# Walking the streamed operand and the accumulator of a matmul in blocks of 16 words, from the last to the first

## The chip, the core and the metric

The kernel runs on one core of a Trainium2 chip. A core has a matrix engine (TensorE, PE in the profile, with its weight loads shown apart as PEld), VectorE (DVE), ScalarE (ACT), GpSimd (POOL) and a queue for DMA transfers (SP). On-chip memory has 128 partitions; so has the accumulator memory of the matrix engine, which has eight banks of 512 words of 32 bits in each partition. The metric is the device time of one execution in microseconds, as the median of several runs.

## What is computed

A linear attention without a softmax is followed by two matrix products with a softplus between them, all in 32-bit floats:

```python
# q, k, v: (8, 8, 576, 64)
kv = np.einsum('bhsd,bhse->bhde', k, v)
out = np.einsum('bhsd,bhde->bhse', q, kv)
rms = np.sqrt(np.mean(out * out, axis=-1, keepdims=True) + 1e-06)
attn = out / rms * g_norm
x = attn.transpose(0, 2, 1, 3).reshape(4608, 512)
h = x @ w_in                                    # w_in (512, 2048)
g = np.maximum(h, 0.0) + np.log1p(np.exp(-np.abs(h)))
return g @ w_out                                # w_out (2048, 512)
```

## The kernel before

**Precision by three terms.** TensorE runs in the format `fp32r`, which keeps fewer bits than a 32-bit float. So each operand of the two large products is split into a high part, a scaled low part and a third term that combines both (on ScalarE and VectorE), and three matmuls, added up in the accumulator, stand for one of full precision. That is the loop `for m in range(3)` that appears in each product.

**Two halves of the span.** In the first 357 us the attention is computed and, beside it, the first part of `d_ff` in the plain form: for blocks of 384 tokens, the first product at L858 (twelve matmuls of 384 columns), softplus, split, and the second product at L865 (nine matmuls of 512 columns). From about 357 us on, the rest of `d_ff` is computed in a form that works on blocks of 512 tokens and pairs of 128-row chunks of `d_ff`; this is where the change is.

**The seven-product form.** For a block of 512 tokens and a pair of chunks the first product is a product of 2 x 2 blocks. `wide_step` computes it with seven products of sums and differences of blocks in place of eight (the scheme of Strassen and Winograd). `product(u, q)` is one of the seven: `u` names the combination of the weights (`forms[p][f]`) and of the tokens (`unit_slots`), `q` one of four quarters X, V, Y, Z of two accumulator banks, each 256 words of a partition (`place(q)`). A product is six matmuls at L1060, three terms by two halves of the contraction, each with weights of 128 x 128 and a streamed operand of 128 x 256. The weights differ in every matmul, so each has its own weight load. There are 48 steps of seven products with six matmuls each: 2016 matmuls.

**Who reads the quarters.** Between the products, ScalarE copies a quarter to another one (L1101, L1105) so that the next product adds onto it, or to on-chip memory (L1084); ScalarE applies softplus to finished quarters (L1087), and VectorE adds two quarters and a kept one (L1109). The result is split into its three terms (L1117, L1120, L1123) and goes to the second product at L1130: groups of three matmuls with 512 columns, whose weights are the token data (`gv`, `g`) and whose streamed operand is the split `w_out` (`pieces` and others).

**The streamed operand of L1060.** The token combinations are made by `units_of`: loaded from DRAM, subtracted where needed (L984), split by L1020, L1023 and L1026 into a tile of three terms, up to two combinations, two contraction halves and 256 tokens. The tiles are called `units`, `early` and `turned` in the profile. `dst.tile[:, m, v, kd]` is 256 neighbouring words of each partition. The weights are in `pieces`, `w12` to `w14` and `half0` to `half2`. Two small unused tiles, `gap0` and `gap1`, shift the tiles behind them.

**What sets the order.** The kernel describes its work as tasks for the class `Plan`, each with an engine, an estimated duration (710 ns for a product, 700 for three matmuls of L1130), a position, what it waits for and which buffers it takes and gives back. `Plan.order` simulates this list once and writes out all instructions in the order found. The durations are constants in the code. Each engine then works through its own queue in that order, with semaphores between engines.

Of the kernel before, what the change touches and what calls it, by code (L numbers as in the profile page):

```python
# [18 lines left out]
P = 128  # L19
# [7 lines left out]
def shaped(x, shape, dtype):  # L27

    n = 1
    for d in shape[1:]:  # L30
        n *= d
    words = n // 2 if dtype == BF16 else n
    x = x[:, :words]
    if x.dtype != dtype:
        x = x.bitcast(dtype)
    names = "abcdef"[:len(shape) - 1]
    if len(names) < 2:
        return x
    return x.rearrange(f"r ({' '.join(names)}) -> r {' '.join(names)}", **dict(zip(names, shape[1:])))


class Slot:
# [159 lines left out]
def kernel(  # L202
# [24 lines left out]
    nc = tc.nc  # L227
# [80 lines left out]
    minus_r = space("gv1", 4 * WIDE, False, F32R)[:, 3 * NT:3 * NT + P]  # L308
    early = space("early", 2 * PIECE, False)
    kvs = [shaped(early[:, 2 * PIECE - (i + 1) * NP * D:2 * PIECE - i * NP * D], [P, NP, D], F32) for i in range(2)]  # L310
    tails = [shaped(space("g0", 2 * WIDE, False)[:, i * H * D:], [P, H, D], F32) for i in range(2)]

    rings = dict(m=8, n=9, e=4, xv=2, gv=2, g=2, raw=1, rawb=1, sq=1, tail0=1, tail1=1, qa=1, xb=1, x=2, r=2,
# [12 lines left out]
    def new(s, shape, dtype=F32):  # L326
# [4 lines left out]
        elif r == "ab":  # L331
            s.tile = banks[:, 2 * i:2 * i + 2]
        elif bank is not None:
            s.tile = shaped(banks[:, bank], shape, dtype)
        elif r == "xv":
            s.tile = shaped(units[:, 3 * i:3 * i + 3].rearrange("r a b -> r (a b)"), shape, dtype)
# [701 lines left out]
    def wide_step(k):  # L1038
        ph, n, p = STEPS[k]
        ab, gv = slot("ab"), slot("gvp")  # L1040
        b = starts[k]
# [6 lines left out]
        def place(q):  # L1048
            return ab.tile[:, q // 2, q % 2 * HW:(q % 2 + 1) * HW]
# [3 lines left out]
        def product(u, q):  # L1053
            f, i = PRODUCTS[u]
            w = forms[p][f].tile
            dst, v = unit_slots[ph, n, u]
            for m in range(3):
                for kd in range(2):
                    at = i * 2 * P + kd * P
                    nc.tensor.matmul(place(q), lhsT=w[:, m, at:at + P], rhs=dst.tile[:, m, v, kd] if u < 6 else dst.tile[:, m, kd],  # L1060
                                     start=(u == 0 and not m and not kd), stop=(m == 2 and kd == 1), skip_group_check=True)

        def multiply(u, q, after, pos, take=(), follows=None):
            f = PRODUCTS[u][0]
            give = [unit_slots[ph, n, u][0]] if last else []
            if final and u in (2, 3, 5, 6):
                give.append(forms[p][f])
            return add("PE", 710, lambda: product(u, q), unit_done[ph, n, u] + forms_done[p][f] + list(after), pos, take, give,
                       follows=follows)
# [19 lines left out]
        def begin():  # L1089
            new(ab, None)  # L1090
            product(0, X)
# [168 lines left out]
```

## Time and profile before

| | |
|---|---|
| Median of 3 runs | 868.56 us (868.41 to 869.19) |
| Span of the profiled execution | 867.5 us, 17041 instructions |
| TensorE, matmuls busy | 853.9 us (98%), 6464 matmuls |
| TensorE, weight loads busy | 760.3 us (88%) |
| VectorE, ScalarE, GpSimd busy | 704.4, 521.3, 76.6 us |
| Matmuls of L1060 | 2016, 128 x 256, 282 to 283 ns recorded for each |
| Matmuls of L1130 | 1152, 128 x 512, 389 to 394 ns recorded for each |
| Moved by DMA | 167.07 MB, mean 193 GB/s |

The profiled execution is one of its own; the profile gives its span, from the first to the last instruction, and the runs behind the median are timed as whole executions. The recorded time of one matmul runs from its start to the modelled arrival of its last result. Consecutive matmuls overlap, so the sum of the recorded times is larger than the time they take, and the distance from start to start is what a matmul costs in a row of them. A line of the timeline has the start in us from the span's start, the time from the first start to the last end of the instructions merged in it, the engine, the line, the operation, the tiles written and read, the shapes and the count. In a line of the waits stand who waited, for whom, the sum of the waiting in us, how often, and the longest.

### The profile page before, as it was taken

What the parts mean: (1) busy time and instruction counts of PE and PEld (TensorE: products, weight loads), DVE (VectorE), ACT (ScalarE), POOL (GpSimd) and SP (SyncE); (2) the same over time, 40 slices, a digit from 0 to 9 for tenths busy, and PEclk for the clock granted to TensorE, in tenths of its full rate; (3) what the DMA queues carried; (4) which work ended last, traced back from release to release, by engine and by line L of the source; (5) the groups of instructions that cost most, each with busy time, mean ns of one, the idle gap of its engine ahead of it and who ended that gap; (6) DMA issues with size and microseconds to landing.
All of it is one profiled execution on the core that took longest, in us unless ns stands there. A gap on an engine that the chain in (4) does not pass through costs nothing.

```text
span 867.5 us, 17041 instructions
## 1 busy us (share of the span) xinstructions
PE 853.9 (98%) x6464; PEld 760.3 (88%) x6464; DVE 704.4 (81%) x995; ACT 521.3 (60%) x980; POOL 76.6 (9%) x79
## 2 busy tenths in 40 slices
PE   7899999999999999999999999999999999999998
PEld 5678888898888999989999999998999899999996
DVE  7888898888788879798887798878788666788873
ACT  6866664445444467766667655654868555566654
POOL 0342223111113200000000000000000000000000
PEclk9999999999999999999999999999999999999999
DMA  9998998779773655436645546545364752777764
GB/s 278 285 242 230 244 262 255 172 224 234 211 188 114 180 175 166 145 108 209 210 156 164 168 151 205 188 144 170 122 201 140 230 165 91 241 236 241 242 190 126
DMA packets 239778, 167.07 MB, mean 193 GB/s; under 512 B 106320, under 2 KB 198736, under 8 KB 239696
## 3 DMA queue, kind: packets, MB, share of 16 engines
q1 hardware_dynamic: 239392, 165.86, 64.5%
q8 instruction: 50, 0.82, 0.4%
q14 instruction: 32, 0.26, 0.1%
q10 hardware_dynamic: 304, 0.13, 0.1%
HBM read 112.98 MB, written 52.95 MB: 191 GB/s over the span
## 4 chain that ended last, share of the span: by engine, by line
PE 94%; DVE 1%; ACT 1%; POOL 0%; issue 0%; ACTq 0%; DVEq 0%
PE banks L1130 31%; PE banks L1060 28%; PE banks L865 16%; PE banks L858 15%; PE banks L715 2%; PE banks L691 2%; PE banks L733 0%; DVE units L638 0%; DVE half L727 0%; PE banks L1224 0%; POOL roots L723 0%; DVE units L641 0%; DVE roots L719 0%; DVE m L459 0%; ACT units L635 0%
## 5 line engine op out<-in xcount | busy, mean ns | idle before, releaser
L1130 PE MATMUL banks<-pieces,gv 128*128 128x512 f32 x768 | 239.9, 394 | 0.0
L1130 PEld LDWEIGHTS banks<-pieces,gv 128*128 128x128 f32 x768 | 133.5, 189 | 18.4
L1130 PE MATMUL banks<-pieces,g_False 128*128 128x512 f32 x384 | 149.4, 389 | 0.0
L858 PE MATMUL banks<-units,pieces 128*128 128x384 f32 x768 | 145.4, 337 | 0.0
L865 PE MATMUL banks<-pieces,gv 128*128 128x512 f32 x576 | 144.9, 396 | 0.0
L858 PEld LDWEIGHTS banks<-units,pieces 128*128 128x128 f32 x768 | 135.5, 188 | 4.8
L865 PEld LDWEIGHTS banks<-pieces,gv 128*128 128x128 f32 x576 | 106.1, 188 | 20.3
L1060 PEld LDWEIGHTS banks<-units,pieces 128*128 128x128 f32 x840 | 112.8, 190 | 6.8 <-ACT banks L1105 0.4
L1060 PE MATMUL banks<-units,pieces 128*128 128x256 f32 x840 | 117.1, 282 | 0.0
L880 ACT ACTIVATE half<-banks 128x384 f32<-128x384 f32 x64 | 31.4, 491 | 98.2 <-PE banks L858 98.0
L1120 DVE TENSOR_TENSOR gv<-g_True,gv 128x1024 fp32r<-128x1024 f32 x47 | 57.5, 1223 | 37.8 <-ACT gv L1117 37.8
L1130 PEld LDWEIGHTS banks<-pieces,g_False 128*128 128x128 f32 x384 | 72.2, 188 | 15.9
L1060 PEld LDWEIGHTS banks<-units,w 128*128 128x128 f32 x504 | 67.8, 190 | 3.9 <-ACT banks L1105 0.2
L1060 PE MATMUL banks<-units,w 128*128 128x256 f32 x504 | 70.7, 282 | 0.0
L723 POOL TENSOR_TENSOR roots<-roots,half 128x8 f32<-128x8 f32 x36 | 62.3, 1731 | 3.0
L1123 DVE SCALAR_TENSOR_TENSOR g_False<-gv 128x1024 fp32r<-128x1024 f32 x47 | 57.6, 1225 | 1.5
L1109 DVE TENSOR_TENSOR g_True<-banks,g_True 128x512 f32<-128x512 f32 x48 | 33.1, 690 | 30.5 <-PE banks L1060 24.5
L1087 ACT ACTIVATE g_True<-banks 128x256 f32<-128x256 f32 x96 | 36.6, 382 | 32.8 <-PE banks L1060 32.2
L1023 DVE TENSOR_TENSOR units<-loads,units 128x1024 fp32r<-128x1024 f32 x42 | 51.2, 1219 | 6.3 <-ACT units L1020 6.3
L925 ACT ACTIVATE m<-banks 128x512 f32<-128x512 f32 x72 | 42.1, 595 | 19.8 <-PE banks L1130 13.8
L1026 DVE SCALAR_TENSOR_TENSOR units<-units 128x1024 fp32r<-128x1024 f32 x42 | 51.4, 1224 | 1.8
L869 DVE TENSOR_TENSOR gv<-half,gv 128x384 fp32r<-128x384 f32 x64 | 35.4, 553 | 20.6 <-ACT gv L882 19.9
(115 smaller groups left out, 1260.5 us busy)
## 6 DMA issues: line engine op xcount, KB each, us to landing
loads<-x SPq DMA_DIRECT2D x180, 128.0 KB, 2.6
part<-m SPq DMA_DIRECT2D x72, 256.0 KB, 2.9
m<-part SPq DMA_DIRECT2D x72, 256.0 KB, 3.2
loads<-form SPq DMA_DIRECT2D x45, 256.0 KB, 3.2
form<-loads SPq DMA_DIRECT2D x36, 256.0 KB, 3.0
raw<-in_moe_w_in_dram SPq DMA_DIRECT2D x16, 512.0 KB, 4.5
loads<-in_k_dram SPq DMA_DIRECT2D x32, 256.0 KB, 4.1
loads<-in_v_dram SPq DMA_DIRECT2D x32, 256.0 KB, 4.4
```

The costliest lines, as they stand in the source:

```text
L723: nc.gpsimd.tensor_tensor(out=r.tile, in0=r.tile, in1=half, op=ALU.pow)
L858: nc.tensor.matmul(hp, lhsT=w_in.tile[:, i, kd * P:(kd + 1) * P], rhs=xv.tile[:, i, kd], start=(m == 0), stop=(m == 3 * KD - 1))
L865: nc.tensor.matmul(mine[i].tile, lhsT=gv.tile[:, m, i * P:(i + 1) * P], rhs=w_out.tile[:, m], start=(c == cs[0] and m == 0), stop=(c == cs ...
L869: nc.vector.tensor_tensor(out=gv.tile[:, 1], in0=g.tile, in1=gv.tile.bitcast(F32)[:, 0], op=ALU.subtract)
L925: a = add("ACT", 690 if ph == LAST else 600, lambda: nc.scalar.activation(new(ot, [P, d_model]), bank.tile, func=AF.Copy, scale=scale if p ...
L1023: nc.vector.tensor_tensor(out=part_of(1, F32R), in0=xl.tile if m > 1 else xl.tile[:, 0], in1=part_of(0), op=ALU.subtract)
L1026: nc.vector.scalar_tensor_tensor(out=part_of(2, F32R), in0=part_of(1), scalar=-RADIX, in1=part_of(0), op0=ALU.mult, op1=ALU.add)
L1060: nc.tensor.matmul(place(q), lhsT=w[:, m, at:at + P], rhs=dst.tile[:, m, v, kd] if u < 6 else dst.tile[:, m, kd], start=(u == 0 and not m ...
L1087: nc.scalar.activation(dst, src, func=AF.Softplus, scale=1.0 + E)
L1120: nc.vector.tensor_tensor(out=gvt(1, F32R), in0=gt(), in1=gvt(0), op=ALU.subtract)
L1123: nc.vector.scalar_tensor_tensor(out=gt(F32R), in0=gvt(1), scalar=-RADIX, in1=gvt(0), op0=ALU.mult, op1=ALU.add)
L1130: nc.tensor.matmul(mine[i].tile, lhsT=(gvt(m, F32R) if m < 2 else gt(F32R))[:, c, i * P:(i + 1) * P], rhs=outs[c].tile[:, m], start=fresh ...
```

## The change

Each matmul of `product` reads its streamed operand, and writes its result, in another order. The 256 words of a partition are seen as 16 blocks of 16 words; the blocks are taken from the last to the first, and the words inside a block stay in rising order. The streamed operand and the result are permuted alike, so every word of the result stands at the same address as before, and is the same sum. The weights, the accumulation, the shapes (128 x 16 x 16 in place of 128 x 256) and the other products, L858, L865 and L1130, are not touched.

```diff
+def from_the_end(x):
+
+    return x.rearrange("p (b w) -> p b w", w=16)[:, ::-1]
...
             for m in range(3):
                 for kd in range(2):
                     at = i * 2 * P + kd * P
-                    nc.tensor.matmul(place(q), lhsT=w[:, m, at:at + P], rhs=dst.tile[:, m, v, kd] if u < 6 else dst.tile[:, m, kd],
+                    nc.tensor.matmul(from_the_end(place(q)), lhsT=w[:, m, at:at + P],
+                                     rhs=from_the_end(dst.tile[:, m, v, kd] if u < 6 else dst.tile[:, m, kd]),
                                      start=(u == 0 and not m and not kd), stop=(m == 2 and kd == 1), skip_group_check=True)
```

## The prediction

> **What bounds the kernel now.** I read the page's first lines, then its chain, then the windows and timeline of the second half. Engine shares, then the granted clock (the program has one core):
>
> ```profile
> PE 853.9 (98%) x6464; PEld 760.3 (88%) x6464; DVE 704.4 (81%) x995; ACT 521.3 (60%) x980; POOL 76.6 (9%) x79
> ...
> PEclk9999999999999999999999999999999999999999
> ...
> PE 94%; DVE 1%; ACT 1%; POOL 0%; issue 0%; ACTq 0%; DVEq 0%
> ```
>
> TensorE is busy 98% of the span at a clock that is never cut, and 94% of the chain that ended last is TensorE. A busy share alone says little, because matmuls overlap; so I look at the chain from 357 us on, where the seven-product form runs, and at who waits there:
>
> ```profile
> by line: PE banks L1130 51.9%; PE banks L1060 46.9%; PE banks L865 0.4%; DVE m L918 0.1%; ACT m L915 0.1%; PE banks L946 0.0%; PE banks L1173 0.0%; issue 0.0%
> ...
> 360.12 8.63 PE banks L1060 x72
> ```
>
> ```profile
> ACT banks L1105 <- PE banks L1060: 49.5, 33, 3.1
> ...
> PEld banks L1060 <- ACT banks L1105: 0.6, 3, 0.2
> ```
>
> 98.8% of the last 510 us are two lines of matmuls that follow each other, the changed L1060 and the second product's L1130. The others wait for TensorE (ScalarE's copy L1105 49.5 us for L1060 alone); the wait the other way is 0.6 us. So what a matmul of L1060 gains or loses goes into the span one for one, as far as other engines keep up. 46.9% of 510.5 us over 2016 matmuls is 118.8 ns for one; the 72 in a row give 8630 / 72 = 119.9. I take 119.4 between them, 2016 x 0.1194 = 240.7 us. One nanosecond on each of the 2016 is 2.0 us of the time, 0.23%.
>
> What one matmul costs is read from starts, since the recorded 282 ns overlap. TensorE's timeline:
>
> ```profile
> 503.31 1.59 PE L1060 MATMUL banks<-units,pieces 128*128 128x256 f32 x12
> 504.74 0.63 PE L1130 MATMUL banks<-pieces,gv 128*128 128x512 f32 x2
> 505.21 0.39 PE L1130 MATMUL banks<-pieces,g_False 128*128 128x512 f32 x1
> 505.44 0.87 PE L1060 MATMUL banks<-early,pieces 128*128 128x256 f32 x6
> 506.15 0.88 PE L1060 MATMUL banks<-turned,half 128*128 128x256 f32 x6
> 506.87 1.60 PE L1060 MATMUL banks<-units,w 128*128 128x256 f32 x12
> 508.31 0.63 PE L1130 MATMUL banks<-pieces,gv 128*128 128x512 f32 x2
> ...
> 510.37 0.62 PE L1130 MATMUL banks<-pieces,gv 128*128 128x512 f32 x2
> ...
> 511.05 0.88 PE L1060 MATMUL banks<-units,w 128*128 128x256 f32 x6
> ```
>
> Settled runs: 508.31 - 506.87 = 1.44 us for twelve of 256 columns, 120.0 ns each; 511.05 - 510.37 = 0.68 us for three of 512, 226.7 each. Between them a column costs 106.7 / 256 = 0.417 ns, and 120.0 - 256 x 0.417 = 13.3 ns is left that does not depend on the columns. Two departures matter. After a run of 512-column matmuls, L1060 is quicker than settled (505.44 to 506.15: 118; 503.31 to 504.74: 119.2). After a run of L1060, the first three of L1130 take 504.74 to 505.44, 0.70 us, or 233 each, and only later 226.7. Something between two matmuls, or between a matmul and the weight load beside it, moves by several nanoseconds at the same column count. That is the only quantity that this change can touch.
>
> **The change part by part.** All 2016 matmuls of L1060 get, for the streamed operand and for the accumulator, a pattern of 16 blocks of 16 words, last block first, in place of 256 words in a row. Columns, weights, data, banks and semaphores stay. The instructions of all five engines' queues stand in the same order in the built program as before; nothing is added, removed or moved, and no wait is new. The planner's cost of a product (710 ns) is a constant, so the order cannot react.
>
> *The streaming itself:* 256 columns by 0.417 ns either way, difference 0, if a step from block to block is free.
>
> *The 15 steps back inside each stream.* No matmul of before steps backwards by blocks. The nearest row is L1224, whose stream is one block of 128 words read four times, so three jumps in 512 columns (its output runs straight):
>
> ```profile
> 16.52 1.09 PE L1224 MATMUL banks<-ident_r 128*128 128x512 f32 x4
> ```
>
> ```profile
> 43.53 1.08 PE L1224 MATMUL banks<-ident_r 128*128 128x512 f32 x4
> ```
>
> Taking off one recorded matmul (0.39, as L1130's), three starts take 0.70 and 0.69 us: 233 and 230 each, against 226.7. Lower end 0: L1130, with no jump, also shows 233 after L1060. Upper end (233 - 226.7) / 3 = 2.1 ns for a jump, by 15, 31 ns for a matmul, 64 us in all. I take 0, since the excess is no larger than in the row without jumps, and put the upper end in a rival. A jump in the accumulator has no row; the same two ends serve.
>
> *The meeting of stream and weight load.* Each matmul streams while the next one's 128x128 weights are read from the same memory (LDWEIGHTS busy 88%, 186 to 192 ns each). Both now run upwards; afterwards the stream runs down by blocks and the weights up. From below: L1060 after long matmuls. Its quickest stretch above is 118, so -1.4 ns; if all of the 13.3 ns were such a meeting and half of it went, as much as -6.7. From above: the first three of L1130 after L1060, 6.3 ns over settled; by 2016, +12.7 us. Between the ends, what lines pay over their settled value on average: L1130 51.9% x 510.5 / 1152 = 230.0, that is +3.3; L865 (nine in 2.08 us, 231.1) +4.4; L858 (twelve in 2.10 us, 175.0, against 384 x 0.417 + 13.3 = 173.3) +1.7. L1060 alone settles without excess. I take that it loses this and pays what L1130, its neighbour on the same engine, pays: 120.0 + 3.3 = 123.3, 3.9 ns over 119.4, **+7.9 us**.
>
> *Readers of the result* (L1101, L1105, L1087 on ScalarE, L1109 on VectorE) find the same words at the same addresses, and wait for the last matmul as before: 0. Their 49.5 and 32.2 us of waiting cover a later product.
>
> Sum: the profiled execution spans 867.5 us; the median of the runs shown is 868.56, 1.1 us more. 868.6 + 7.9 = 876.5; forecast **876 us**, slower by 0.9%.
>
> The Trainium skill, SBUF — State Buffer, section Door 1, speaks against the change more strongly: memory is read in lines of 16 bytes, the accumulator has lines of 8 bytes, and "any non-contiguous PSUM access pattern significantly slows down matmuls". Blocks of 64 bytes keep whole lines, so by its mechanism the sum stays at 868.6, while its sentence taken literally gives the last rival below; no row here writes the accumulator in blocks. The same skill, TensorE: Matmul & The Clock Gate, "Step-by-step", says that weights and stream have separate read ports and that loading the next weights takes nothing from the running matmul; by that the meeting costs 0, again 868.6. The 0.70 against 0.68 us above does not settle it.
>
> **The rivals.**
>
> *Nothing happens* (the walk is free, and the memories see the same lines): 868.6 us. For it: where the two streams' relative position changes, at the switches between lines, the start-to-start stays within a few nanoseconds; L1060 is 119 to 120 ns over `units`, `early` and `turned` alike. Against it: the 6.3 ns excess exists and needs a cause.
>
> *Faster.* The 13.3 ns beyond the columns is, in part, the stream stalling behind a weight load that goes the same way, and opposite directions meet only shortly. One mechanism, at L1060; it decides if more than 0.9 ns a matmul goes (1.7 us in all). Half the 13.3 ns would give 113 ns: 2016 x (119.4 - 113.3) = 12.3 us, **856 us**. At 113 ns ScalarE's copies could come late (its wait for L1060 is 0.6 us now), so I do not go lower. For it: L1060 does run below settled after long matmuls. Against it: the 13.3 ns is the same at 256 and 512 columns and at each relative position, as a fixed hand-over would be.
>
> *Each step costs.* 15 steps at one column time, 0.417 ns, are 6.3 ns, 12.6 us, 881; at two column times 25.2 us, 894; at the upper end of L1224, 933. Against it: L1224's excess is shared by rows without jumps.
>
> *The accumulator takes blocks at half rate.* 256 more column times, 106.7 ns a matmul, 215 us: 1084 us. Nothing in the trace speaks for it; the skill's sentence above is its only ground.
>
> **How the numbers follow.** Forecast (the meeting costs, 870.5 to 882) 0.35; faster 0.29; nothing 0.24; steps cost 0.09; half rate 0.03. 0.2% is 1.7 us, about what a measurement of this kernel can tell from no change. Faster 0.29, same 0.24, slower 0.35 + 0.09 + 0.03 = 0.47. The range reaches down to 854, a little below the faster case, and up to the two-column step's 894; outside lie the half rate, the dearest steps, and tails of the others, under 0.2.
>
> **What the profile after would show.** The same counts on each line, L1060's shapes in blocks. Forecast right: twelve of L1060 in about 1.48 us, L1060's share of the last stretch up, L1130 as before, others' waits for L1060 longer. Nothing: 1.44 again. Faster: 1.36, and idle time at L1060 for L1105. Wrong in its ground: if L1060 stays at 120 and L1130 or the switches change, the meeting is not within the product but in what it leaves to its neighbours.

## The result, and the profile after

The changed kernel takes 866.46 us (median of 8 runs, 865.16 to 868.08), the kernel before 868.89 us (8 runs beside it). The ratio is 0.9966, with a 95% interval of 0.9956 to 0.9977: faster by 0.34%, about 2.9 us (the ratio is not the quotient of the two medians, which lie 2.4 us apart). The forecast was 876 us, slower by 0.9%.

The lines of the file have moved by five or six: L1060 is now L1065, L1130 is L1136, L1105 is L1111, L1087 is L1093, L1109 is L1115. The page of the changed kernel, shares and chain:

```profile
PE 851.7 (98%) x6464; PEld 758.6 (88%) x6464; DVE 704.5 (81%) x995; ACT 520.8 (60%) x980; POOL 76.1 (9%) x79
...
PE 93%; DMA 3%; DVE 2%; ACT 1%; POOL 1%; SPq 0%; issue 0%; DVEq 0%; ACTq 0%
```

Counts are the same, and TensorE still carries the chain. Its chain over the form (window from 356 us on), changed kernel; a piece has its start in us, its time, and what it is:

```profile
by line: PE banks L1136 51.7%; PE banks L1065 46.5%; PE banks L870 1.0%; ACT m L920 0.1%; DVE m L923 0.1%; PE banks L951 0.0%; PE banks L1179 0.0%; issue 0.0%
...
361.97 8.53 PE banks L1065 x72
...
756.53 4.24 PE banks L1065 x36
```

72 matmuls in a row take 8.53 us where they took 8.63, 118.5 ns each in place of 119.9. The 36 in a row take 117.8 ns each. Who waits, in the same window:

```profile
ACT banks L1111 <- PE banks L1065: 50.0, 32, 3.2
```

ScalarE waits for the form as long as before (50.0 us against 49.5), and the form's weight loads wait for ScalarE's copies 0.6 us, as before; so nothing else has become the bound. TensorE's timeline in one step of the changed kernel:

```profile
507.78 1.58 PE L1065 MATMUL banks<-units,w 128*128 128x256 f32 x12
509.19 0.62 PE L1136 MATMUL banks<-pieces,gv 128*128 128x512 f32 x2
...
509.88 0.62 PE L1136 MATMUL banks<-pieces,gv 128*128 128x512 f32 x2
...
511.26 0.62 PE L1136 MATMUL banks<-pieces,gv 128*128 128x512 f32 x2
...
511.94 0.28 PE L1065 MATMUL banks<-units,w 128*128 128x256 f32 x1
```

Twelve matmuls of the form take 509.19 - 507.78 = 1.41 us (117.5 ns each), where twelve took 1.44. The second product's threes take 0.69, 0.69, 0.69 (509.19 to 511.26) and 0.68 us, where they took 0.69, 0.69, 0.68, 0.68. These are two more lines of the kernel before; the others of that step, at 508.31, 510.37 and 511.05, stand in the prediction:

```profile
509.00 0.63 PE L1130 MATMUL banks<-pieces,gv 128*128 128x512 f32 x2
...
509.69 0.62 PE L1130 MATMUL banks<-pieces,gv 128*128 128x512 f32 x2
```

From here on four numbers describe a kernel, all from the recorded starts of its trace. "Form" is the distance from start to start averaged over the 2016 matmuls of the form; distances over 160 ns, where TensorE waited, are left out (over 265 ns for the lines with more columns). "Settled" is the average over those matmuls of the form that follow at least six others of it. "Second product" is the distance averaged over the 1152 matmuls of L1130. "Stretch" is the time from the first start of the form, which in the kernel before is at 338.9 us, while the plain form still runs, to the last start of a matmul.

| | form, ns | settled, ns | second product, ns | stretch, us |
|---|---|---|---|---|
| before | 119.27 | 119.98 | 230.0 | 524.4 |
| changed | 118.12 | 117.78 | 229.2 | 521.3 |

2016 x 1.15 = 2.3 us come from the form itself and 1152 x 0.8 = 0.9 us from the second product, whose code is the same. Together they are about the 3.1 us of the stretch. The profiled execution shows only 1.3 us of it (span 866.2 against 867.5): it reached the form 1.8 us later. The windows of the first 50 us show a likely reason. Kernel before, busy time of the engines, then the granted clock:

```profile
0.00:50.00 50.00, 41.43 (x524) 30.34 (x525) 42.19 (x74) 34.76 (x67) 13.39 (x19) 1.00 1.01 273
```

Changed kernel:

```profile
0.00:50.00 50.00, 41.02 (x517) 30.40 (x518) 41.28 (x73) 33.84 (x65) 13.19 (x19) 0.97 0.97 270
```

The clock fell to half for 3.4 us (26.4 to 29.8 us), which can cost up to 1.7 us. Such falls come and go: the mean granted clock of single executions of the kernel before was 0.996 to 1.000. So the experiments below are judged by the stretch and by the distances, not by one time.

### The profile page after: what moved, and what is told of

It is laid out like the page before. It is cut to its first block, busy times and chain, and to the rows that moved or that the text cites. A ratio compares the mean times of both kernels' runs of the same rounds, so it can differ in the third digit from the quotient of the medians.

```text
span 866.2 us, 17080 instructions
## 1 busy us (share of the span) xinstructions
PE 851.7 (98%) x6464; PEld 758.6 (88%) x6464; DVE 704.5 (81%) x995; ACT 520.8 (60%) x980; POOL 76.1 (9%) x79
## 4 chain that ended last, share of the span: by engine, by line
PE 93%; DMA 3%; DVE 2%; ACT 1%; POOL 1%; SPq 0%; issue 0%; DVEq 0%; ACTq 0%
PE banks L1136 30%; PE banks L1065 28%; PE banks L870 15%; PE banks L863 15%; PE banks L720 2%; PE banks L696 2%; DMA loads<-in_v_dram 1%; DMA raw<-in_moe_w_in_dram 1%; PE banks L738 0%; PE banks L1230 0%; POOL roots L728 0%; DVE half L732 0%; SPq L766 0%; DVE units L643 0%; ACT w L802 0%
## 5 line engine op out<-in xcount | busy, mean ns | idle before, releaser
L1136 PE MATMUL banks<-pieces,gv 128*128 128x512 f32 x768 | 238.1, 391 | 0.0
L1136 PE MATMUL banks<-pieces,g_False 128*128 128x512 f32 x384 | 150.6, 392 | 0.0
L1136 PEld LDWEIGHTS banks<-pieces,gv 128*128 128x128 f32 x768 | 132.6, 188 | 17.8
L1065 PEld LDWEIGHTS banks<-units,pieces 128*128 128x128 f32 x840 | 112.0, 188 | 6.6 <-ACT banks L1111 0.4
L1065 PE MATMUL banks<-units,pieces 128*128 128x256 f32 x840 | 116.4, 282 | 0.0
L1136 PEld LDWEIGHTS banks<-pieces,g_False 128*128 128x128 f32 x384 | 71.9, 187 | 16.5
L1065 PEld LDWEIGHTS banks<-units,w 128*128 128x128 f32 x504 | 67.3, 188 | 3.8 <-ACT banks L1111 0.2
L1065 PE MATMUL banks<-units,w 128*128 128x256 f32 x504 | 70.3, 282 | 0.0
L1115 DVE TENSOR_TENSOR g_True<-banks,g_True 128x512 f32<-128x512 f32 x48 | 33.1, 691 | 28.4 <-PE banks L1065 23.1
L1093 ACT ACTIVATE g_True<-banks 128x256 f32<-128x256 f32 x96 | 36.7, 383 | 31.8 <-PE banks L1065 31.2
L1025 ACT ACTIVATE units<-loads 128x1024 fp32r<-128x1024 f32 x42 | 44.4, 1057 | 13.4 <-PE banks L1065 10.4
```

The costliest lines, as they stand in the source:

```text
L1025: nc.scalar.activation(part_of(0, F32R), xl.tile if m > 1 else xl.tile[:, 0], func=AF.Copy, scale=DOWN)
L1065: nc.tensor.matmul(from_the_end(place(q)), lhsT=w[:, m, at:at + P], rhs=from_the_end(dst.tile[:, m, v, kd] if u < 6 else dst.tile[:, m, kd ...
L1093: nc.scalar.activation(dst, src, func=AF.Softplus, scale=1.0 + E)
L1136: nc.tensor.matmul(mine[i].tile, lhsT=(gvt(m, F32R) if m < 2 else gt(F32R))[:, c, i * P:(i + 1) * P], rhs=outs[c].tile[:, m], start=fresh ...
```

## The experiments

Theory A: the stream of a matmul and the load of the next one's weights read from the same on-chip memory and hinder each other, and the order of the stream's reads decides how much. Theory B: the order of the accumulator's writes decides. Theory C: a pattern with several dimensions behaves otherwise, whatever its direction. Later, A2: the stream's own walk counts, whatever the weights do.

### Reading and writing apart

```diff
-nc.tensor.matmul(from_the_end(place(q)), lhsT=..., rhs=from_the_end(dst.tile[...]),
+nc.tensor.matmul(place(q), lhsT=..., rhs=from_the_end(dst.tile[...]),       # e1
+nc.tensor.matmul(from_the_end(place(q)), lhsT=..., rhs=dst.tile[...],       # e2
```

> Only the streamed operand of the seven-product form is read from the last block to the first; the result is written straight, so the tokens of each block of 256 come out in another order (the same amount of work). Before, a matmul of this form costs 119.3 ns from start to start on average and exactly 120 in long runs; with both walks changed, 118.1 on average and 118, 119, 116 in turn. Theory A (the stream and the load of the next weights meet in the on-chip memory, and the direction of the read decides): 118.1 and the same turn of three, as if nothing had been left out. Theory B (the accumulator's addresses decide): 119.3 and a steady 120. Theory C (the shape of the pattern decides, not its direction): between, or 118.1 here and in every other run with a pattern of blocks.

> Only the result is written from the last block to the first; the streamed operand is read straight, so the tokens of each block of 256 come out in another order (the same amount of work). Theory A (reading decides): 119.3 ns on average, steady 120 in long runs, as before. Theory B (the accumulator decides): 118.1, in turns of 118, 119, 116.

Reading alone: 118.13 ns, settled 117.78, second product 229.2, stretch 521.2 us; one run took 866.26 us beside 870.59 of the kernel before. Writing alone: 119.26, 119.98, 230.0, 524.4; 868.74 us. The chains, reading alone:

```profile
360.36 8.48 PE banks L1065 x72
574.60 4.25 PE banks L1065 x36
```

Writing alone:

```profile
359.41 8.63 PE banks L1065 x72
575.12 4.31 PE banks L1065 x36
```

The kernel before:

```profile
575.82 4.31 PE banks L1060 x36
```

The 36 in a row take 4.25 us with the read turned and 4.31 with only the write turned, as before. B falls: the whole effect is in the read. The Trainium skill, SBUF — State Buffer, section Door 1, says that any non-contiguous access to the accumulator slows matmuls significantly; 16 blocks written backwards cost nothing here (119.26 against 119.27 ns).

### Other walks with the same blocks

```diff
-    return x.rearrange("p (b w) -> p b w", w=16)[:, ::-1]
+    return x.rearrange("p (b t w) -> p t b w", t=2, w=16)      # e3: even blocks, then odd ones, upwards
+    return x.rearrange("p (b w) -> p b w", w=1)[:, ::-1]       # e4: word by word
```

> Both walks in blocks of 16 words again, but upwards: first the even blocks, then the odd ones. Theory A (direction against the weight load): not 118.1; 119.3 as before, or some ns more, as the stream now passes the same places twice at double speed. Theory C (a pattern of two or more dimensions as such): 118.1.

> Both walks go from the last word to the first, one word at a time, 256 steps of -1. Theory A: 118.1 with the same turn of three, since the direction over the memory is the same as with blocks of 16, if a backward step inside a line of memory is free; if it is not, clearly more than 120 (a word that needs an access of its own would cost tens of ns). Theory C: one dimension again, so 119.3.

Even and odd: the form 120.11 ns, slower than before, settled 120.01; but the second product 226.8 and the stretch 522.5 us, less than before. Word by word: 118.20, settled 118.48, second product 228.0, stretch 520.0 us, better than the change itself. Single runs took 866.11 and 864.88 us beside 870.59. With even and odd blocks A's "119.3 or some ns more" held, and C's 118.1 did not come: a pattern of several dimensions does not give it, while the single words, one dimension, do. C falls. With single words A's 118.1 came out on average, but not its turn of 118, 119, 116. No expectation named that a walk can pay at the neighbour. The second product's first two matmuls after the form cost 233 and 236 ns before; after the even-odd walk they are at 226 and 227 at once. A run of twelve of the second product after 24 matmuls of the form, kernel before:

```profile
445.30 2.75 PE banks L1130 x12
```

Even and odd:

```profile
443.83 2.72 PE banks L1136 x12
```

240 more steps back in each matmul moved the form by 0.08 ns on average (118.20 against 118.12; settled 118.48 against 117.78), so a single backward step has next to no cost.

### Moving the weights against the streams

An unused tile, `gap1`, lies between the streamed operands and all weights of the form. Widened, it moves the weights and leaves the streams.

```diff
-    SHIFT = 64
+    SHIFT = 128      # 256 bytes further; e5 with the walk upwards as before, e6 downwards as changed
+    SHIFT = 80       # 64 bytes further; e9 upwards, e10 downwards
```

> The kernel before (stream upwards), with the unused tile in front of the weights widened from 64 to 128 words: all weights of the seven-product form lie 256 bytes further on against the streamed operands, which stay where they are. Theory A (the stream's reads get in the way of the load of the next weights, or it in theirs): the relative place of the two counts, so the 119.3 ns of the form or the settled 120 move, by half a nanosecond or more, here or in the next run. Theory A2 (the stream's reads alone count, whatever the weights do, as at the border of two matmuls): 119.3 and 120.0 as before.

> The changed kernel (stream down in blocks of 16), with the same 256 bytes more in front of the weights. Theory A: the 118.1 ns, or the turn of 118, 119, 116, change. Theory A2: 118.1 and the same turn.

256 bytes change nothing: 119.28, settled 119.99, second product 230.0, stretch 524.4 us upwards, 118.12, 117.78, 229.2, 521.2 downwards. By what was written beforehand A had fallen and A2 stood (the single runs, 869.48 and 866.38 us, stood beside 868.72). But a memory whose parts repeat every 256 bytes or less would not notice such a step, so a smaller one was tried:

> The kernel before (stream upwards) with the weights 64 bytes further on against the streams, a quarter of the step that changed nothing. Theory A (stream and weight load hinder each other where both are in the same part of the memory): if the parts repeat every 256 bytes, the step of 256 was blind and this one moves the settled 120.0 ns or the second product's 230.0 by half a nanosecond or more. Theory A2 (the stream's own walk counts, or the pace of the weight load by itself): 119.3, 120.0 and 230.0 again.

> The changed kernel (down in blocks of 16) with the same 64 bytes. Theory A: another turn than 118, 119, 116 or another mean than 118.1 ns. Theory A2: the same.

With 64 bytes and the old walk, the form falls to 115.75 ns, settled 113.92, and the stretch to 516.3 us, 8.1 less than before and 5.0 less than with the change. One run took 861.69 us beside 870.59. With the changed walk the same step gives 118.02 ns, settled 117.76, other turns of values (mostly 120, 115 and 118 in place of 116, 119 and 118), and 230.1 at the second product: 522.1 us, worse than without the step, by the second product (870.72 us, with the clock at half three times in the first 60 us). The chain of the kernel with 64 bytes, walk upwards:

```profile
360.37 8.48 PE banks L1065 x72
572.61 4.11 PE banks L1065 x36
```

And with the changed walk:

```profile
578.48 4.24 PE banks L1065 x36
```

4.11 us for 36 is 114.2 ns each; 4.24 us is what the changed kernel took without the step. A2 falls: for the walk upwards, the place of the weights decides. For the walk from the end only the turn of values moves; its settled average was 117.8 with 0, 64 and 256 bytes.

### Half of the weight load

```diff
-nc.tensor.matmul(place(q), lhsT=w[:, m, at:at + P], ...
+nc.tensor.matmul(place(q)[:P // 2], lhsT=w[:, m, at:at + P // 2], ...   # e11; e12 with both walks turned
```

> Stream upwards as before, but each matmul of the seven-product form loads only the first 64 of its 128 weight columns, and so computes only half of its result (the other 64 partitions of each quarter keep what they had). The stream is as long as before, 256 columns or 106.7 ns. If the weight load sets the form's pace or hinders the stream, the 119.3 ns fall, to 113 or less; if the 13.3 ns beyond the columns are a hand-over that does not depend on the load's length, 119 to 120 stays.

> The same half of the weights with the changed walk (down in blocks of 16; half of the result is left out again). Theory A: with half the load the two walks meet half as often; what is gained by the change (1.2 ns a matmul) shrinks, and both walks come to within half a nanosecond of each other. Theory A2 (the walk alone): down stays 1.2 ns or more below up.

The weight loads in the first of the two kernels, from the groups of the profile:

```profile
L1136 PEld LDWEIGHTS banks<-pieces,gv 128*128 128x128 f32 x768 | 132.0, 188 | 18.4 <-DVE banks L909 0.2
...
L1065 PEld LDWEIGHTS banks<-units,pieces 128*64 128x64 f32 x840 | 99.6, 134 | 10.9 <-ACT banks L1111 0.4
```

The form's whole load in the kernel before, then in the changed kernel:

```profile
L1060 PEld LDWEIGHTS banks<-units,pieces 128*128 128x128 f32 x840 | 112.8, 190 | 6.8 <-ACT banks L1105 0.4
```

```profile
L1065 PEld LDWEIGHTS banks<-units,pieces 128*128 128x128 f32 x840 | 112.0, 188 | 6.6 <-ACT banks L1111 0.4
```

Half the columns take 134 ns in place of 188 to 190, so 64 columns are 54 to 56 ns: by these lengths the load takes a column every 0.84 to 0.88 ns, about half as fast as the stream with its estimated 0.417. The load is also recorded 2 ns longer in the kernel before than in the changed one, so stream and load are both slower there. The runs of 36, half load upwards:

```profile
571.72 4.09 PE banks L1065 x36
```

Half load, from the end:

```profile
572.73 4.24 PE banks L1065 x36
```

Upwards the form falls to 114.10 ns, settled 113.40, and the stretch to 513.7 us (859.98 us). Downwards it is 117.77 and 117.81, as with the whole load (520.3 us, 863.94). So of the settled 120 ns of the kernel before, 6.6 go with the load's columns from 64 on. Half a load also writes only half of the result's partitions, and this run alone does not tell the two apart; the 64-byte step, which leaves both whole, takes away nearly as much (6.1).

For the walk from the end both expectations missed: the two walks did not come within half a nanosecond of each other, nor did down stay below up. Down lies 4.4 ns above up and does not notice the missing half. What the changed walk has left over the 113.4 does not come from these columns, and no run here shows where it comes from. The Trainium skill, TensorE: Matmul & The Clock Gate, "Step-by-step", says that loading the next weights takes no read bandwidth from the running matmul; upwards, where half a load saved 5.2 ns a matmul on average and 6.6 settled, these runs do not agree.

### Period, and relative or absolute place

```diff
-    SHIFT = 64
+    SHIFT = 80       # e13, timed
+    SHIFT = 96       # e14: 128 bytes;  112: 192 bytes (e15);  72: 32 bytes (e17);  88: 96 bytes (e18)
-    const.tile([P, 8], F32, name="gap0")
+    const.tile([P, 24], F32, name="gap0")     # e16, with SHIFT = 64: everything 64 bytes further
```

> The first unused tile is widened by 64 bytes, so the streamed operands, the weights and all other tiles of the large products move on together by 64 bytes; stream upwards. Theory A (only the relative place of stream and weights counts): 119.3 ns, 120.0 settled, 230.0 at the second product, as before. If instead the place of one of them in the memory counts by itself, 115.8 as with the weights alone moved, or a third value.

The form 119.27 ns, settled 119.98, the second product 230.0, the stretch 524.4 us: the kernel before to the last digit. Streams and weights moved together keep their pace, so it is their relative place that counts. (Its one run, 872.02 us beside a median of 869.41, reached the form 2.7 us later, in part by a half-clock interval of 3.4 us.) That the other engines' reads and writes set the pace is unlikely: in the kernel before 992 of the 1007 settled distances are 120 ns, whatever the others do. The chain:

```profile
362.82 8.63 PE banks L1065 x72
578.52 4.31 PE banks L1065 x36
```

> Weights 128 bytes further on than before, stream upwards. With 0, 64 and 256 bytes measured (120.0, 113.9, 120.0 ns settled), theory A says that the value depends on the step modulo 256 bytes or less; if the parts repeat every 128 bytes, 128 gives 120.0 again, else something between 113 and 127. Theory A2 had fallen with the step of 64.

> Weights 192 bytes further on, stream upwards. If the parts repeat every 128 bytes, 113.9 ns settled as with 64; if every 256, a value of its own, between 113 and 127.

> Weights 32 bytes further on than before, stream upwards. Measured so far for steps of 0, 64, 128, 192 and 256 bytes: 119.3, 115.7, 119.1, 117.8 and 119.3 ns in the seven-product form. If the memory's parts are 64 bytes wide, half a part moves the meeting by half a step: a value between 115.7 and 119.3 and a time between 861 and 869 us. If narrower parts count, anything between 113 and 123.

> Weights 96 bytes further on, stream upwards. With parts of 64 bytes: between the 115.7 ns of 64 and the 119.1 of 128, and a time between 861 and 873 us.

All with the old walk upwards:

| weights further by, bytes | form, ns | settled, ns | second product, ns | stretch, us |
|---|---|---|---|---|
| 0 | 119.27 | 119.98 | 230.0 | 524.4 |
| 32 | 118.52 | 118.19 | 232.5 | 526.0 |
| 64 | 115.75 | 113.92 | 229.2 | 516.3 |
| 96 | 118.13 | 118.20 | 233.0 | 525.7 |
| 128 | 119.10 | 119.15 | 232.2 | 526.8 |
| 192 | 117.79 | 117.67 | 233.4 | 525.4 |
| 256 | 119.28 | 119.99 | 230.0 | 524.4 |

The values repeat after 256 bytes and not after 64, 128 or 192. The kernel before lies at the worst of the places tried. The four places 64 bytes apart average 117.7 ns settled upwards, close to the 117.8 that the walk from the end kept with 0 and 64 bytes. That would fit a stream which passes the load at all relative places in turn when it runs the other way; this is an argument, and no run tests it. 64 is no flat optimum; 32 bytes on either side lose most of it, and the second product goes its own way, since the same step moves its streams against its weights. The expectations for 32 and 96 bytes held in the form and missed in the time: 872.14 us (ratio 1.0024, 1.0013 to 1.0034) and 873.52 us (1.0039, 1.0026 to 1.0052), slower than before, because the second product lost more than the form gained, and the 512-column line of the plain form lost too (232.0 and 233.1 ns against 230.7). Steps of 128 and 192 took 875.0 and 872.26 us in one run each.

### The best version, timed

> The kernel of the 64-byte step once more (stream upwards, nothing of the change), timed. One look had 115.8 ns in place of 119.3 in the seven-product form and a last stretch of 516.3 us in place of 524.4. Theory A (relative place): 8 us less than the kernel before, a ratio of 0.990 to 0.992.

861.04 us against 869.41 us, ratio 0.9906, 0.9889 to 0.9922, as expected. The form 115.69 ns, settled 113.73, stretch 516.2 us. It has nothing of the change in it and beats both kernels.

### The walk in all lines

```diff
-nc.tensor.matmul(mine[i].tile, lhsT=..., rhs=outs[c].tile[:, m], ...
+nc.tensor.matmul(from_the_end(mine[i].tile), lhsT=..., rhs=from_the_end(outs[c].tile[:, m]), ...
```

and likewise in the two lines of the plain form; e7 with blocks of 16, e8 word by word.

> Blocks of 16 from the last to the first in all four lines of large matmuls: the two of the plain form (384 and 512 columns) and the second product (512) as well. If a meeting of stream and weight load is what is shortened, each line can gain: the plain form's 175.5 and 230.7 ns and the second product's 229.2 come nearer to 173.3 and 226.7, at most 768 x 2.2 + 576 x 4.0 + 1152 x 2.5 = 6.9 us less than the changed kernel. If the gain of the change comes from the 256-column rhythm alone, the other lines stay or lose.

> As the run before, but word by word from the last to the first in all four lines. In the seven-product form this gave a stretch of 520.0 us in place of 521.2, mostly at the second product (228.0 in place of 229.2 ns). Theory A: at least as good as blocks in all lines; if single words lose where the stream has no slack (512 columns), 2 ns or more above blocks there.

Both are slower than before: 873.69 and 876.16 us in one run each, beside 868.72. With blocks, the plain form's matmuls of 384 columns go from 175.5 to 177.1 ns, those of 512 from 230.7 to 233.2, and the second product's to 233.3, though the seven-product form, at 117.79 on average, is a little quicker than with the change alone. Word by word the lines are no better (178.1, 233.4 and 233.3, the form 118.57), against the expectation that words do at least as well as blocks. Walking down is no gain as such; among these lines it gained only in the one of 256 columns, where the walk upwards stood at its worst place.

## Why the prediction was wrong

*What bounds the kernel* held. The chain stayed on TensorE, ScalarE's and VectorE's waits for the form hardly moved, and nanoseconds per matmul came out as microseconds of the stretch: 2.3 + 0.9 against 3.1.

*The streaming itself, and the steps back*, taken at 0, held as far as the runs can tell: writing 16 blocks backwards cost nothing (119.26 against 119.27 ns), and reading 256 single words took as long as 16 blocks to within 0.1 ns on average (0.7 settled). The upper end from L1224 (2.1 ns a jump) was far off. So the rival in which each step costs is not borne out: in the lines of 512 columns, which did get slower, words and blocks were equally slow (233.3 and 233.3).

*The meeting of stream and weight load* is the step that failed. That the two meet is what the runs show; the sign of what the turned walk does to it was wrong. It was put at +3.9 ns a matmul, because L1060 "alone settles without excess" and would come to pay what its neighbours pay. It measured -1.15 ns. The settled 120.0 ns were read as the columns and a fixed hand-over of 13.3 ns, since 226.7 at 512 columns left the same remainder. The runs show that 6.1 to 6.6 of these 13.3 ns go with the meeting: with half the load 113.40, with the weights 64 bytes further 113.92. So L1060 did carry an excess, hidden by its steadiness, and the change took 1.2 ns of it on average and 2.2 settled. The sign was there to read: the distances under the settled value just after long matmuls (118) said that 120 is not a floor. The 0.417 ns a column were worked out from the same two settled values, so this split of columns and remainder is an estimate too; how much of the remainder at 512 columns is a meeting, no run shows.

*The rival "faster"* had the mechanism, "the stream stalling behind a weight load", and 113.3 ns as its price. The change reached 1.2 ns of the 6.1 that it reckoned with; the 64-byte step came nearly to the price, but only settled (113.9; 115.7 on average). Its size was wrong for this change. That 113.3 is so near the settled floor of two other experiments is luck, since half of the 13.3 ns was a guess. Its reason, that opposite walks meet only shortly, was not tested: which way the load walks is not shown by any run.

*The rival "nothing"* was backed by the switches between lines, where the relative place of stream and weights changes and the pace does not. By the tile sizes in this kernel these changes are multiples of 256 bytes, the very step that the runs show to be blind. *The accumulator at half rate* fell with the run in which only the write was turned.

*The second product* was to stay as before. It gave 0.9 of the 3.1 us. Wrong in its ground was named for the case that the form stays at 120 and the second product or the switches change; here both changed. How the form's walk reaches into the next line was not explained.

Open remains how wide the parts of the memory are within the 256 bytes and which reader yields. The turns of three (118, 119, 116 ns), the pattern of the seven steps, and why the walk from the end keeps its 117.8 ns with half a load and at other places of the weights were not explained. It was not tried to turn the weights' own walk, nor to place the second product's tiles apart from the form's.

## What to carry to other kernels

A steady distance from start to start that fits "columns plus a constant" at several widths is not yet a floor: move the stationary operands by 64 bytes against the streams, or halve the load, before calling the constant a hand-over. Where matmuls load new weights each time, the relative place of the two operands in a partition, modulo 256 bytes, is a free parameter that was worth 0.9% here, more than the order of the walk (0.34%); it has to be scanned, and lines need not share their best value (at 192 bytes the plain form's 384-column line fell from 175.5 to 174.0 ns, while the second product rose to 233.4). Judge such a change by distances in the trace, and look at the neighbours: a line's pace can change with what the line before it does.

## What was not expected of the hardware

- With the walk upwards, the pace of a matmul of 256 columns depends on the relative address of its stream and its weights, and comes back after 256 bytes: 113.9 to 120.0 ns settled over seven places. With the walk in blocks from the end it was 117.8 ns with 0, 64 and 256 bytes, and with half a load.
- The pace of a line of matmuls depends on the line before it: the second product cost 230.0 ns after the old walk, 228.0 after words downwards and 226.8 after even and odd blocks, with its own code and addresses unchanged.
- A weight load of 64 columns was recorded with 134 ns, one of 128 with 188 to 190: 0.84 to 0.88 ns a column.
- The order in which a matmul writes its 256 results in the accumulator made no difference (119.26 against 119.27 ns).
